# Moving one load and one request to another queue and another moment, with fewer filler matmuls, in the first wave of an attention + MLP kernel

## The chip, the cores and the metric

The kernel runs on one core of a Trainium2 chip. A core has five engines that run side by side, each with its own list of instructions: TensorE (PE, matrix products; "PEld" is its weight load), VectorE (DVE), ScalarE (ACT), GpSimd (POOL) and SyncE (SP, which only issues DMAs here). Sixteen DMA engines move data between the device's memory (HBM) and the core's on-chip memory (SBUF); matrix products land in PSUM. A DMA can be asked for by SP (its requests go through the queue that the profile calls q1, "hardware dynamic") or by POOL (q0, "software dynamic"). The metric is the device time in microseconds (us); the median of several runs counts.

## The reference

Two stages. The first is linear attention with decay over 4 batches, 8 heads, 768 positions and head size 64, in blocks of 64 positions: inside a block the scores are masked by powers of the head's decay, and between blocks a 64 x 64 state per head carries on.

```python
intra = (q_b @ k_b^T * Dmask) @ v_b
inter = (q_b * lam_pow) @ kv_state
out_b = intra + inter
kv_state = lam_block * kv_state + (k_b * rev_pow)^T @ v_b
```

The second is an MLP on the 3072 tokens of width 512 that come out, with 2048 hidden units:

```python
h = x @ w_in
g = h * sigmoid(1.702 * h)
out = g @ w_out
```

All inputs and the output are float32; the kernel computes its products in bfloat16.

## The kernel before, in words

The 768 positions of the four batches are worked off in waves, each of which gives 512 tokens to the MLP. Waves 0 and 1 (`w < ND`) are "dense": each takes 256 positions of two batches, called `c` = 0 and 1 (batch 0 and batch 1 in wave 0). Waves 2 to 5 take 128 positions of all four batches. While the MLP of one wave runs on TensorE, the attention of the next one is threaded in between.

`load_one` (L76) loads one of q, k, v of one batch in a wave, on SP's queue: 512 KB in rows of 512 B, either whole or in two halves by heads (L79). `load(0)` at L104 asks for all of wave 0, in the order k, q, v of batch 0, then k, q, v of batch 1; of these only v of batch 1 comes as a whole. The two weight matrices are loaded once, by `load_w_in` (L175, five chunks, the first two of 256 columns and three of 512) and `load_w_out` (L180, four chunks), on POOL's queue; these DMAs also turn float32 into bfloat16. As POOL is one engine with one list, its requests stand in line with its own work: casts of k of batch 1 (L480), half of the cast of v of batch 1 (L499), and the later requests for weights (L481, L500 to L503).

When a request goes out is set by hand. `gate_pool(x)` (L451) is a copy of one element of `x` on POOL: it waits until the DMA that brings `x` has landed, and so all that POOL has to do behind it waits too. `gate_sync` (L454) does the same for SP: a tiny DMA that reads `w_out_sb[1]` (L506), behind which `load(1)`, the loads of wave 1, stands.

`fill(n)` (L139) issues n matmuls of zeros, 128 x 128 by 128 x 512, whose result nobody reads. They take up TensorE's time at the start, where it would otherwise wait.

The order of the first wave is written out by hand from L457 on: powers of the decay on ScalarE, then for k and q of batch 0 a multiplication by the powers (`do_cast`, L189, line 198 in the profile), turns by TensorE (`turn_pe`, L228, line 234) with a copy out of PSUM (lines 214 and 217, for VectorE and ScalarE), then the scores (`d_scores`, L247, lines 255 and 263), the state (`d_one` and `d_state`, line 275) and the output (`d_out`, line 312, and `d_inter`, line 294). Batch 1 follows in the same way from L479 on. `mlp1_half(0, 0, 0)` (L509, line 405) is the first product with `w_in`, from its first chunk; the rest of wave 0's MLP follows in lines 405, 393 and 417.

After this the list `main` (L545) holds the MLP's pieces and `side` the attention's, each with the place in `main` ahead of which it is issued. Wave 1's k cast stands ahead of piece 19 of wave 0's MLP and its turn ahead of piece 24.

Of the kernel before, what the change touches and what calls it, by code (L numbers as in the profile page):

```python
# [24 lines left out]
def kernel(  # L25
# [13 lines left out]
    nc = tc.nc  # L39
    f32 = mybir.dt.float32  # L40
    bf16 = mybir.dt.bfloat16
    B, H, S, D = q.shape
# [31 lines left out]
    loaded = {}  # L74

    def load_one(w, c, nm, src):  # L76
        x = ld.tile([P, H, 2 * D], f32, tag=f"{nm}{c}", name=f"{nm}f")
        if w < ND:
            n = H if w or (nm == "v" and c) else H // 2  # L79
            for h in range(0, H, n):  # L80
                nc.sync.dma_start(  # L81
                    out=x[:, h : h + n],
                    in_=src[2 * w + c, h : h + n, 0 : 2 * P, :].rearrange("h (s a) d -> s h (a d)", a=2))
        else:
            nc.sync.dma_start(out=x.rearrange("p h (a d) -> p (h a) d", a=2),
                              in_=src[2 * c : 2 * c + 2, :, w * P : (w + 1) * P, :].rearrange("b h s d -> s (b h) d"))
        loaded[w, c, nm] = x

    def load(w, nms="kqv"):
        src = {"k": k, "q": q, "v": v}  # L90
        if w < ND:
            for c in range(HF):
                for nm in nms:
                    load_one(w, c, nm, src[nm])
        else:
            for nm in nms:
                for c in range(HF):
                    load_one(w, c, nm, src[nm])
# [3 lines left out]
    ones = const.tile([1, P], f32)  # L102
    nc.vector.memset(ones, 1.0)
    load(0)  # L104

    nc.scalar.preload_act_table_set("natural_log_exp_and_others")
# [29 lines left out]
    def acc(name, dt=f32, shape=None, tag="a"):  # L136
        return ps.tile(shape or [P, 4, P], dt, tag=tag, bufs={"a": 5, "mm": 3}[tag], name=name)

    def fill(n, new=None):  # L139
        if new:  # L140
            fill_ps[0] = acc("ps_fill", shape=[P, W], tag=new)
        for _ in range(n):
            nc.tensor.matmul(fill_ps[0], zero[:, 0:P], zero, start=True, stop=True)  # L143
# [31 lines left out]
    def load_w_in(j):  # L175
        c0 = sum(IN_CH[:j]) * P
        nc.gpsimd.dma_start(
            out=w_in_sb[j], in_=moe_w_in.rearrange("(kc ki) f -> ki kc f", ki=P)[:, :, c0 : c0 + IN_CH[j] * P])
# [10 lines left out]
    def do_cast(w, c, nm, eng, g=None):  # L189
        if g in (None, 0):  # L190
            cast[w, c, nm] = work.tile([P, 2, HD], bf16, tag=f"{nm}s{c}", name=f"{nm}s")
        f, x = loaded[w, c, nm], cast[w, c, nm]
        if w < ND:
            pw = {"k": kd_pow, "q": qd_pow}[nm]
            for R in (0, 1) if g is None else (g,):
                for j in range(2):
                    h = slice(4 * R + 2 * j, 4 * R + 2 * j + 2)
                    eng.tensor_tensor(x.rearrange("p a (r i j d) -> p r j i a d", i=2, j=2, d=D)[:, R, j],  # L198
                                      f[:, h].rearrange("p i (a d) -> p i a d", a=2),
                                      pw[:, h].unsqueeze(3).to_broadcast([P, 2, 2, D]), op=MUL)  # L200
        else:
            pw = {"k": k_pow, "q": q_pow}[nm]
            n = 2 * H // 4
            for j in range(2):
                eng.tensor_tensor(x.rearrange("p b (r i j d) -> p j (b r) i d", i=2, j=2, d=D)[:, j],  # L205
                                  f.rearrange("p h (a d) -> p (h a) d", a=2).rearrange("p (n j i) d -> p j n i d", j=2, i=2)[:, j],
                                  pw.rearrange("p b (r j i) -> p j (b r) i", i=2, j=2)[:, j].unsqueeze(3).to_broadcast([P, n, 2, D]),
                                  op=MUL)
# [10 lines left out]
    def cast_v(w, c, copies=(pool_copy, pool_copy)):  # L219
        f = loaded.pop((w, c, "v"))  # L220
        dst = v_sb[w % 2]
        if w < ND:
            for a in range(2):
                copies[a](dst[:, 2 * c + a], f.rearrange("p h (a d) -> p h a d", a=2)[:, :, a, :])
        else:
            copies[0](dst[:, 2 * c : 2 * c + 2].rearrange("p b h d -> p (b h d)"), f.rearrange("p h e -> p (h e)"))

    def turn_pe(w, c, nm, copy=act_copy, g=None):  # L228
        x = cast[w, c, nm]
        rr = list(range(NP)) if g is None else [2 * g, 2 * g + 1]  # L230
        t = acc("ps_t", bf16, [P, len(rr), 2, P])
        for i, r in enumerate(rr):
            for a in range(2):
                nc.tensor.transpose(t[:, i, a, :], x[:, a, r * P : (r + 1) * P], ident)  # L234
        if g in (None, 0):
            trans[w, c, nm] = work.tile([P, 2 * NP, P], bf16, tag=f"{nm}T{c}", name=f"{nm}T")
        copy(trans[w, c, nm][:, 2 * rr[0] : 2 * rr[0] + 2 * len(rr)], t.rearrange("p r a s -> p (r a) s"))
# [9 lines left out]
    def d_scores(w, c, pp, split=False):  # L247
        kT = trans[w, c, "k"]
        s2 = [acc("ps_s") for _ in range(2)]
        for i in range(2):  # L250
            r = 2 * pp + i
            for a in range(2):
                for blk, bs in enumerate((A, Z)):
                    for h, hs in enumerate((A, Z)):
                        nc.tensor.matmul(s2[h][bs, 2 * i + a, :], kT[hs, 2 * r + a, bs], q_of(w, c, hs, r, blk),  # L255
                                         start=True, stop=True)
        for h in range(2):
            sm = work.tile([P, 2, 2, P], bf16, tag="sm", bufs=8, name="sm")
            flat = s2[h].rearrange("p (i a) s -> p i (a s)", i=2)
            if split and h:  # L260
                nc.scalar.copy(sm.rearrange("p i a s -> p i (a s)"), flat)
                flat = sm.rearrange("p i a s -> p i (a s)")
            nc.vector.tensor_tensor(sm.rearrange("p i a s -> p i (a s)"), flat,  # L263
                                    mask_d.rearrange("p o a b s -> p o (a b s)").to_broadcast([P, 2, 2 * P]), op=MUL)
            masked[w, c, pp, h] = sm
# [185 lines left out]
    def gate_pool(x):  # L451
        nc.gpsimd.tensor_copy(behind_q, x)
# [4 lines left out]
    with tc.manual_schedule():  # L457
# [4 lines left out]
            nc.scalar.activation(blk_pow[rows].rearrange("p (r i) -> p r i", i=2),  # L462
                                 ln_lam[rows].rearrange("p (r j i) -> p r j i", i=2, j=2)[:, :, j, :], EXP, scale=1.0 * P)
        nc.scalar.activation(warm, q_pow[:, 0, 0:1], GELU)
        fill(5)
        for nm, copies in (("k", (dve_copy, act_copy)), ("q", (act_copy, dve_copy))):
            for g in range(2):
                do_cast(0, 0, nm, nc.vector, g)
            for g in range(2):
                turn_pe(0, 0, nm, copies[g], g)  # L470
                fill(2 if nm == "k" or g == 0 else 0)
        gate_pool(loaded[0, 0, "v"][0:1, 0, 0:1])
        load_w_in(0)
        cast_v(0, 0, (act_copy, act_copy))
        d_scores(0, 0, 0)
        fill(1)
        d_scores(0, 0, 1)
        fill(3)
        for g in range(2):  # L479
# [22 lines left out]
        for j in range(NCH):  # L502
            load_w_out(j)  # L503
        nc.gpsimd.affine_select(mask, mask, pattern=[[0, 1], [1, P]], channel_multiplier=-1, base=0,
                                compare_op=mybir.AluOpType.is_ge, fill=0.0)
        gate_sync(w_out_sb[1][0:1, 0, 0:2])  # L506
        load(1)
        d_scores(0, 1, 1, True)
        mlp1_half(0, 0, 0)  # L509
# [98 lines left out]
```

## Time and profile before

| | us |
|---|---|
| median of 5 runs | 208.13 |
| lowest and highest | 207.39, 209.78 |
| profiled execution, its own time | 208.47 |
| its span, first to last instruction | 206.8 |
| TensorE busy | 199.1 (96%) |
| VectorE busy | 89.5 (43%) |
| ScalarE busy | 86.2 (42%) |
| GpSimd busy | 16.2 (8%) |
| DMA queue of SP, share of 16 engines | 56.8% |
| DMA queue of GpSimd, share of 16 engines | 13.1% |

The times in a timeline count from the span's first instruction. A row of a chain or a timeline begins with start and duration; a bracket with an arrow tells how long the engine stood idle before, and what ended that. In a row of a DMA queue stand the packets, the megabytes written, and the time that the packets took as a share of 16 engines, which can be over 100% as packets overlap. A request for a DMA on SP or POOL has a duration too: it is the time of issuing, not of moving the data; the landing is told apart from it. Busy time of TensorE counts a matmul until its modelled end, so an engine that is 96% busy isn't at 96% of its peak.

### The profile page before, as it was taken

What the parts mean: (1) busy time and instruction counts of PE and PEld (TensorE: products, weight loads), DVE (VectorE), ACT (ScalarE), POOL (GpSimd) and SP (SyncE); (2) the same over time, 40 slices, a digit from 0 to 9 for tenths busy, and PEclk for the clock granted to TensorE, in tenths of its full rate; (3) what the DMA queues carried; (4) which work ended last, traced back from release to release, by engine and by line L of the source; (5) the groups of instructions that cost most, each with busy time, mean ns of one, the idle gap of its engine ahead of it and who ended that gap; (6) DMA issues with size and microseconds to landing.
All of it is one profiled execution on the core that took longest, in us unless ns stands there. A gap on an engine that the chain in (4) does not pass through costs nothing.

```text
span 206.8 us, 4271 instructions
## 1 busy us (share of the span) xinstructions
PE 199.1 (96%) x1806; PEld 104.5 (51%) x1830; DVE 89.5 (43%) x160; ACT 86.2 (42%) x158; POOL 16.2 (8%) x37
## 2 busy tenths in 40 slices
PE   7999999999999999999999999999999999999994
PEld 2477444467854464444464444464444454444453
DVE  1892000686951843931743841743841731100121
ACT  4877661157665030566021566021466021565000
POOL 4369000060000000000000000000000000000000
PEclk9999999999999999999999999999999999999999
DMA  5999999999899899988991379971360011100112
GB/s 146 330 238 178 176 206 239 319 310 227 182 215 172 196 276 245 236 194 196 230 270 71 103 179 229 243 216 52 101 155 0 37 68 51 51 0 0 54 51 101
DMA packets 87640, 33.82 MB, mean 164 GB/s; under 512 B 67398, under 2 KB 84678, under 8 KB 87622
## 3 DMA queue, kind: packets, MB, share of 16 engines
q1 hardware_dynamic: 82868, 29.37, 56.8%
q0 software_dynamic: 4752, 4.19, 13.1%
q8 instruction: 14, 0.23, 0.4%
q14 instruction: 4, 0.03, 0.1%
q10 hardware_dynamic: 2, 0.00, 0.0%
HBM read 27.26 MB, written 6.29 MB: 162 GB/s over the span
## 4 chain that ended last, share of the span: by engine, by line
PE 76%; DMA 15%; SPq 4%; DVE 2%; POOL 1%; issue 1%
PE ps_out L417 35%; PE ps_h L393 28%; DMA w_out<-in_moe_w_out_dram 6%; PE ps_h L405 3%; DMA vf<-in_v_dram 3%; SPq L81 3%; DMA kf<-in_k_dram 3%; PE ps_s L331 2%; PE ps_o L381 2%; DMA qT<-qs 2%; PE ps_o L368 1%; DVE o_sb L421 1%; PE ps_t L234 1%; PE ps_kv L355 1%; DVE ks L198 1%
## 5 line engine op out<-in xcount | busy, mean ns | idle before, releaser
L417 PE MATMUL ps_out<-w_out,g_sb 128*128 128x512 bf16 (+2 forms) x400 | 83.8, 362 | 1.1 <-issue 0.6
L393 PE MATMUL ps_h<-xT,w_in 128*128 128x512 bf16 x330 | 73.2, 379 | 0.3
L395 ACT ACTIVATE g_sb<-ps_h 128x512 bf16<-128x512 f32 x84 | 50.2, 597 | 45.2 <-PE ps_h L393 45.2
L417 PEld LDWEIGHTS <-g_sb 128*128 128x128 bf16 x416 | 38.2, 98 | 41.0
L393 PEld LDWEIGHTS <-w_in 128*128 128x128 bf16 x336 | 32.9, 98 | 39.2
L421 DVE COPY o_sb<-ps_out 128x512 f32<-128x512 f32 (+2 forms) x26 | 16.9, 651 | 52.4 <-PE ps_out L417 52.3
L339 DVE SCALAR_TENSOR_TENSOR sm<-ps_s,inv_pow,mask 128x512 bf16<-128x512 f32 x32 | 21.8, 743 | 27.5 <-PE ps_s L331 27.5
L385 ACT CAST xT<-ps_o 128x512 bf16<-128x512 f32 x16 | 8.2, 599 | 38.1 <-PE ps_o L381 38.1
L198 DVE TENSOR_TENSOR ks<-kf,kd_pow 128x256 bf16<-128x256 f32 x8 | 2.9, 421 | 22.6 <-DMA kf<-in_k_dram 19.3
L405 PE MATMUL ps_h<-xT,w_in 128*128 128x256 bf16 x96 | 11.4, 273 | 0.2 <-DMA w_in<-in_moe_w_in_dram 0.2
L205 DVE TENSOR_TENSOR qs<-qf,q_pow 128x512 bf16<-128x512 f32 x16 | 10.3, 686 | 0.0
L205 DVE TENSOR_TENSOR ks<-kf,k_pow 128x512 bf16<-128x512 f32 x16 | 10.3, 684 | 0.0
L405 PEld LDWEIGHTS <-w_in 128*128 128x128 bf16 x96 | 9.0, 98 | 1.9 <-DMA w_in<-in_moe_w_in_dram 0.4
L263 DVE TENSOR_TENSOR sm<-ps_s,mask_d 128x512 bf16<-128x512 f32 x14 | 8.8, 684 | 0.7 <-PE ps_s L255 0.5
L407 ACT ACTIVATE g_sb<-ps_h 128x512 bf16<-128x512 f32 x12 | 7.2, 598 | 4.3 <-PE ps_h L405 4.3
L143 PE MATMUL ps_fill<-zero 128*128 128x512 bf16 x18 | 6.8, 504 | 1.4 <-DVE zero L113 1.4
L359 DVE SCALAR_TENSOR_TENSOR kv<-kv,blk_pow,ps_kv 128x256 bf16<-128x256 bf16 x12 | 5.0, 477 | 6.0 <-PE ps_kv L355 6.0
L217 ACT COPY kT<-ps_t 128x512 bf16<-128x512 bf16 (+1 forms) x4 | 3.2, 792 | 8.2 <-PE ps_t L234 8.2
L198 DVE TENSOR_TENSOR qs<-qf,qd_pow 128x256 bf16<-128x256 f32 x16 | 5.9, 428 | 0.1
L214 DVE CAST v_sb<-vf 128x1024 bf16<-128x1024 f32 x8 | 5.3, 689 | 1.1 <-DMA vf<-in_v_dram 1.1
L331 PEld LDWEIGHTS <-kT 64*128 64x128 bf16 x128 | 3.6, 94 | 3.6 <-issue 3.6
L331 PE MATMUL ps_s<-qT,kT 64*128 64x128 bf16 x128 | 5.1, 217 | 0.1
(68 smaller groups left out, 90.6 us busy)
## 6 DMA issues: line engine op xcount, KB each, us to landing
vf<-in_v_dram SPq DMA_DIRECT2D x11, 512.0 KB, 6.4
kf<-in_k_dram SPq DMA_DIRECT2D x10, 512.0 KB, 5.6
qf<-in_q_dram SPq DMA_DIRECT2D x10, 512.0 KB, 6.6
out_dram<-o_sb SPq DMA_DIRECT2D x15, 256.0 KB, 2.0
out_dram<-o_sb SPq DMA_DIRECT2D x17, 128.0 KB, 2.4
w_out<-in_moe_w_out_dram POOLq DMA_DIRECT2D x4, 512.0 KB, 14.4
w_in<-in_moe_w_in_dram POOLq DMA_DIRECT2D x3, 512.0 KB, 8.0
kf<-in_k_dram SPq DMA_DIRECT2D x4, 256.0 KB, 3.1
```

Source lines behind the costliest of these rows:

```text
L198: eng.tensor_tensor(x.rearrange("p a (r i j d) -> p r j i a d", i=2, j=2, d=D)[:, R, j], f[:, h].rearrange("p i (a d) -> p i a d", a=2), p ...
L205: eng.tensor_tensor(x.rearrange("p b (r i j d) -> p j (b r) i d", i=2, j=2, d=D)[:, j], f.rearrange("p h (a d) -> p (h a) d", a=2).rearran ...
L263: nc.vector.tensor_tensor(sm.rearrange("p i a s -> p i (a s)"), flat, mask_d.rearrange("p o a b s -> p o (a b s)").to_broadcast([P, 2, 2 * ...
L331: nc.tensor.matmul(s2[h][:, b, :], kT[hs, (b % 2) * NP + p, :], qT[hs, (b % 2) * NP + p, :], start=True, stop=True)
L339: nc.vector.scalar_tensor_tensor(sm, s, inv_pow[:, n : n + 1], mask.to_broadcast([P, B, P]), op0=MUL, op1=MUL)
L385: nc.scalar.copy(xT[w][:, p, :], ps_o.rearrange("p b s -> p (b s)"))
L393: nc.tensor.matmul(h, w_in_sb[j][:, kc, i * P : (i + 1) * P], xT[w][:, kc, :], start=(kc == 0), stop=(kc == KC - 1))
L395: nc.scalar.activation(g_of[w][:, fc, :], h, GELU)
L405: nc.tensor.matmul(h[:, u, :], w_in_sb[j][:, kc, i * P : (i + 1) * P], xT[w][:, kc, cols], start=(kc == 0), stop=(kc == KC - 1))
L407: nc.scalar.activation(g_of[w][:, fc : fc + 2, cols], h, GELU)
L417: nc.tensor.matmul(ps_out, g_of[w][:, fc, g * P : (g + 1) * P], w_out_sb[j][:, fc % CW, c0:c1], start=(fc == 0), stop=(fc == FFC - 1))
L421: nc.vector.tensor_copy(o, ps_out)
```

## The change

Four edits, all of them in wave 0.

1. v of batch 1 is no longer loaded by SP at the start. POOL asks for it, on its own queue, right behind the request for the first chunk of `w_in` and ahead of its casts of k of batch 1.
2. The element that POOL's gate copies is no longer the first of v of batch 0 but the first of the second half of q of batch 0 (`H // 2` is where that half begins).
3. Five fillers go: two of the five ahead of the first turn, one behind the second turn of k, one behind the first turn of q, and the one between the two groups of scores.
4. `load` leaves out the tile that is now asked for by hand. No computation of the output is changed.

```diff
@@ load_one @@
-                nc.sync.dma_start(
+                (nc.gpsimd if w == 0 and c and nm == "v" else nc.sync).dma_start(
                     out=x[:, h : h + n],
@@ load @@
                 for nm in nms:
-                    load_one(w, c, nm, src[nm])
+                    if w or c == 0 or nm != "v":
+                        load_one(w, c, nm, src[nm])
@@ wave 0 @@
-        fill(5)
+        fill(3)
         for nm, copies in (("k", (dve_copy, act_copy)), ("q", (act_copy, dve_copy))):
             for g in range(2):
                 do_cast(0, 0, nm, nc.vector, g)
             for g in range(2):
                 turn_pe(0, 0, nm, copies[g], g)
-                fill(2 if nm == "k" or g == 0 else 0)
-        gate_pool(loaded[0, 0, "v"][0:1, 0, 0:1])
+                fill(2 - g if nm == "k" else 1 - g)
+        gate_pool(loaded[0, 0, "q"][0:1, H // 2, 0:1])
         load_w_in(0)
+        load_one(0, 1, "v", v)
         cast_v(0, 0, (act_copy, act_copy))
         d_scores(0, 0, 0)
-        fill(1)
         d_scores(0, 0, 1)
         fill(3)
```

## The prediction

> **What bounds the kernel now.** First the page's top and busy rows: how much of the span TensorE is not busy.
>
> ```profile
> span 206.8 us, 4271 instructions
> PE 199.1 (96%) x1806; PEld 104.5 (51%) x1830; DVE 89.5 (43%) x160; ACT 86.2 (42%) x158; POOL 16.2 (8%) x37
> ```
>
> PE is idle for 206.8 - 199.1 = 7.7 us: 1.4 before the first filler, about 3 at the tail, which the change doesn't reach, so some 3.3 are left. That is the ceiling of what earlier data can give; fewer fillers can give little besides, as PE mostly waits where they stand.
>
> Then the chain that ended last, in order of time, since the change is in the first 15 us and I must know by which way they reach the end.
>
> ```profile
> 7.95 7.11 DMA vf<-in_v_dram
> 15.05 0.06 issue
> 15.11 0.61 POOL v_sb L211
> 15.72 1.43 POOL w_in L177 x2
> 17.15 0.71 POOL w_out L181
> 17.86 13.43 DMA w_out<-in_moe_w_out_dram
> 31.30 0.02 issue
> 31.31 0.77 SPq L455
> 32.09 0.05 issue
> 32.14 5.81 DMA kf<-in_k_dram
> 37.95 0.02 issue
> 37.97 1.44 DVE ks L198 x4
> 39.41 0.05 issue
> 39.46 0.40 PE ps_t L234 x4
> ```
>
> v of batch 1 lands at 15.05; POOL casts its half, then asks for the late weights; when the second chunk of w_out lands (31.30) SP may load wave 1; its k lands at 37.95, and PE takes the casts up at 39.46. From there the chain is nearly all PE. So PE at 39.46 is the gate: what PE wins before it is lost in waiting unless the DMA chain moves too. How long PE waits there is in the timeline of PE:
>
> ```profile
> 38.79 0.40 PE L234 MATMUL ps_t<-ident,ks 128*128 128x128 bf16 x4
> 39.46 0.40 PE L234 MATMUL ps_t<-ident,ks 128*128 128x128 bf16 x4 [0.27 <-DVE ks L198]
> ```
>
> PE is 0.27 us early. A PE delay up to 0.27 before this point costs nothing; a DMA delay counts whole.
>
> Last the DMA queues, in stretches of half a microsecond: SP's queue moves 323 to 349 packets of 512 B in each from 6.0 to 12.0 (some 690 a us, about 350 GB/s), and the GpSimd queue's first packets are in 11.5 to 12.0, though its first request was issued from 8.08 to 9.03. Between 12 and 15:
>
> ```profile
> q0 software_dynamic: 864, 0.43, 110.2%
> q1 hardware_dynamic: 297, 0.14, 16.9%
> ```
>
> The engines are full from 6 to 31 us but for two dips: 88% at 13.5 to 14.0 (where 120 to 130% stands beside it), and 91% over 17.9 to 19.0 (110 to 120% beside it). In a full queue a reordering wins only such dips: about 0.15 and 0.25 us.
>
> **The change, part by part.**
>
> Fillers. Five of 20 go: two of fill(5), one behind k's second group, one behind q's first, and fill(1) between the scores. Fill(5) ends where transposes start (5.83), while the cast they need is done by 5.45; with three they start at 5.45. The vector engine gains less: kT's copy (6.33) can't start before the four casts end at 6.06, so 0.27; the q casts, 1.42, follow, and the masks start at about 8.8 instead of 9.08. ScalarE is held by its own exponentials and table load until 7.1 and gains about 0.1. So PE's lead from fillers is some 0.3 us, all before the gate at 39.46: worth 0 at the end.
>
> Against it speaks a rule. The fillers' weight loads are 0.42 us apart at 3.72 to 4.98 (3.72, 4.13, 4.55, 4.98), and after 6 us two fillers take 0.59 together, one latency of 0.38 and 0.21: PE's pace doubled between. The granted clock reads 1.00 throughout and shows nothing of it. The Trainium skill ("TensorE: Matmul & The Clock Gate", Part 1: The HAM clock gate) says that the fast clock comes after a busy window of some 3.4 us. With three fillers PE idles from about 5.1 to 5.45. By the row, the pause ahead of lam_p's matmuls (PE's weight loads stood idle 0.84 us before them) kept nothing back, and I take 0. By the rule, at worst another window at half speed: 16 transposes at 0.05 and three fillers at 0.21 more, 1.4 us, of which two groups of four transposes (0.2 each) and two scores (0.2) lie on the path, +0.6; less 0.27 at the gate and the lead below, +0 to +0.3.
>
> The gate on POOL. Before, POOL waits for v's first half, 4.50 us until 7.87. Now for q's second half: issued at 2.41, 4.4 to landing, 6.81. The 1x1 copy moves with it, and w_in0's issue starts 0.21 later, at 7.03, ending at 7.98 (its row: 0.946). Nothing but the weights and k casts is behind this wait on POOL.
>
> v's issue on POOL. The row for its cost is the weight issues, 0.746 to 0.946 us with 528 packets each (4752 over nine). v has 1024 rows of 512 B, so about 1040 packets: 0.75 if the issue is a fixed cost, 1.9 if it goes with packets at the dearest row. I take 1.5: 7.98 to 9.48. POOL's k casts began at 9.45 and had waited 0.42 for k of batch 1: so the cost is 0.03, hidden by that landing. At 1.9 it is 0.4 on POOL and on PE's transposes at 10.70 (ready 10.66, no slack), covered by the 0.27 and the lead. The late w_in requests behind the casts stay at 11.72.
>
> SP's queue. It loses one issue (7.95, 0.69 us). Nothing is behind it there until the wait on w_out at 31.3: worth 0.
>
> When first weights and v arrive. By the rule (the Trainium skill, "DMA: Bandwidth & Descriptors", Queues, rings and completion order) an engine goes round its queues packet by packet, so from about 9 us w_in0 would take half from k and q of batch 1: q's second half, due at 11.6 (6.99 + 4.6), would slip to 13 and its cast (due 12.3) by 0.8, PE by 0.5 after slack. The row says otherwise: no GpSimd packet until 11.5, and SP's queue undiminished. I take the row: k and q as before, and w_in0's packets from 10.9 (3.8 after its issue, as before) to 11.1, when SP's queue drains, v no longer being in it. 528 packets at 330 a us: 1.6 us, until 12.7, and landing some 0.5 later, 13.2 (before: 14.58). Thus the 0.2 us wait of PE for w_in at 14.65 goes. Next v, from 12.7. Its price is the unknown: no 512 B row of the GpSimd queue is in the trace. SP's 512 B rows take 16/690 = 23 ns of an engine; the GpSimd queue's cast rows 16/330 = 48 ns for 1 KB read and 16/195 = 82 ns for 2 KB. Taken as a line these two give 13 + 35 per KB, so 30 ns at 512 B. Bounds: 23 (the bytes alone) and 48 (a GpSimd packet as such); I take 30, from the same queue. So 1040 x 30/16 = 1.95 us, until 14.65, landed near 15.1: where it landed before. ACT's and POOL's v casts, d_one and what follows then keep their places; PE's next wait is v again (15.7).
>
> The sum at the gate. DMA work up to w_out's second chunk: v by GpSimd instead of SP costs 1.95 - 1.50 = 0.45 more engine time; the dip at 13.5 is filled, 0.15 less; the dip at 18 stays, as v and so the requests at 15.7 don't move. 31.30 becomes 31.6, wave 1's k and PE's transposes at 39.46 are 0.3 later. PE arrives earlier and waits longer. From there the chain is PE's own: +0.3. Span 206.8 to 207.1; the profiled run's 208.47 (1.67 around the span) to 208.77, and by the same difference the median 208.13 to **208.4**. A measurement of this kernel (207.39 to 209.78 in five runs) can hardly tell under 1% from no change.
>
> With 23 ns: no extra engine time, both dips filled (v lands by 14.7, the late requests go out 0.4 earlier): -0.4. With 48 ns: 3.1 instead of 1.5 us, +1.6 - 0.15 = +1.4.
>
> **The rivals.**
>
> *v is as cheap on GpSimd as on SP (bytes decide).* For it: GpSimd's 1 KB and SP's 512 B rows both read near 340 GB/s. Against: the line through GpSimd's own rows doesn't pass through SP's. -0.4: 207.7. If the weights were not bound by the engines, v's whole lead of up to a microsecond would pass on: 207.1.
>
> *v's packets on the GpSimd queue are dear.* One mechanism: 48 ns an engine and packet, so v lands at 16.2, after the 15.05 of now; the k load of wave 1 lands 1.4 later and PE stalls at 39.46. It decides as soon as v's packets cost over 26 ns (0.15 us of dip over 65 packets an engine), and makes the kernel slower: 209.5. For it: that queue has never moved 512 B rows here. Against: its packets' time goes with their bytes. With other v-dependent work late, up to 210.3.
>
> *The clock comes late, or k and q are halved by the round.* PE 0.5 later after slack: 208.7.
>
> *The change does nothing*: all of it is before a gate set by total bytes: 208.1, which the likeliest case can't be told from.
>
> **How the numbers follow.** Likeliest, 208.1 to 208.7: 0.45. v cheap, 207.0 to 208.0: 0.28. v dear, 209.0 to 210.5: 0.20. Late clock or halved queue, 208.5 to 209.3: 0.07. A range of 207.3 to 209.7 leaves out the far ends of both, some 0.2 with the scatter of the median. Slower by over 1% is above 210.2: the last part of the dear case and mishaps, 0.08. Faster by over 1%, under 206.05, needs 2 of the 3.3 us idle: 0.03. The rest 0.89.
>
> **What would show it.** Right: w_in's first issue near 7.0, v's on POOL for 1.5 us; k casts on POOL still near 9.5; no GpSimd packet before 10.5; w_in0 landed near 13.2, v near 15.1; w_out's second chunk near 31.6, PE's wait at 39 grown over 0.27. Fillers at 0.21 apart from 6 us on. Wrong: v landed before 14.6 or after 16; k casts on POOL after 10; PE slow after 6.5; or the wait at 39 gone, which would put the bound on PE itself.

## The result, and the profile after

The changed kernel takes 208.55 us (median of 44 runs), and the kernel before 208.55 us (79 runs in the same comparison). The ratio is 1.0009, with a 95% interval of 0.9994 to 1.0024: 0.2 us more, between 0.1 less and 0.5 more. There is no difference that can be measured. The forecast was 208.4, 0.3 us above the 208.13 of before, and it said that so little could hardly be told from no change. The profiled execution took 208.36 us, its span is 206.6 us (before: 208.47 and 206.8).

The page's first rows of the kernel after:

```profile
span 206.6 us, 4263 instructions
PE 199.3 (96%) x1802; PEld 105.1 (51%) x1825; DVE 89.5 (43%) x160; ACT 86.0 (42%) x158; POOL 17.3 (8%) x38
```

With five fillers fewer PE is busy 0.2 us longer. Something on PE got slower; that is looked for below, behind the chain. First the chain that ended last, of the kernel after, in order of time (start, duration, what):

```profile
7.17 0.44 POOL behind_q L453
7.61 0.88 POOL w_in L178
8.49 6.47 DMA vf<-in_v_dram
14.97 0.06 issue
15.03 0.61 POOL v_sb L212
...
17.78 13.59 DMA w_out<-in_moe_w_out_dram
...
32.20 5.83 DMA kf<-in_k_dram
38.03 0.02 issue
38.05 1.44 DVE ks L199 x4
39.49 0.05 issue
39.54 0.40 PE ps_t L235 x4
```

v of batch 1 travels on another queue and lands at 14.97 instead of 15.05. From there every time is that of before to 0.1 us: w_out's second chunk at 31.36 (31.30), the casts of wave 1's k at 38.05 (37.97), PE's turn of them at 39.54 (39.46). The timeline of PE at that place:

```profile
38.87 0.40 PE L235 MATMUL ps_t<-ident,ks 128*128 128x128 bf16 x4
39.54 0.40 PE L235 MATMUL ps_t<-ident,ks 128*128 128x128 bf16 x4 [0.28 <-DVE ks L199]
```

PE still waits for the casts, 0.28 us where it was 0.27.

Where did the time on PE go? The group of the fillers between 5.8 and 9.6 us, in the kernel before and in the kernel after (count, busy us, mean ns of one):

```profile
L143 PE MATMUL ps_fill<-zero 128*128 128x512 bf16 x8 | 2.8, 412 | 0.0
```

```profile
L144 PE MATMUL ps_fill<-zero 128*128 128x512 bf16 x4 | 2.3, 634 | 0.0
```

A filler takes 634 ns while PE is still slow, called cold from here on, and 379 ns once it is quick (the 412 is a mean with one cold filler in it). In the kernel before PE becomes quick near 5.9 us, in the profiled execution of the kernel after only near 9.7. The granted clock is 1.00 in both and does not show it. What each lost and won is seen in PE's timeline of batch 1, here of the kernel after: scores, first product with w_in, and the beginning of PE's long stretch of products.

```profile
14.19 0.79 PE L256 MATMUL ps_s<-qT,kT 64*64 64x128 bf16 x32
14.90 1.05 PE L406 MATMUL ps_h<-xT,w_in 128*128 128x256 bf16 x8
...
17.92 0.83 PE L406 MATMUL ps_h<-xT,w_in 128*128 128x256 bf16 x6
```

Before, these three began at 13.66, 14.65 and 17.83, and the second had waited 0.20 us for w_in:

```profile
14.65 1.05 PE L405 MATMUL ps_h<-xT,w_in 128*128 128x256 bf16 x8 [0.20 <-DMA w_in<-in_moe_w_in_dram]
```

So after, the scores are 0.53 later (the cold pace), w_in is no longer waited for (it landed at 13.6 instead of 14.6), and the long stretch begins at nearly the same time, 17.92. In this pair of profiles a loss and a gain meet; and behind them stands the wait at 39.5, which would have taken a small loss up to 0.28 us, and any gain.

### The profile page after: what moved, and what is told of

The parts are those of the page before. It is cut to its first block, busy times and chain, and to the rows that moved or that the text cites. A ratio compares the mean times of both kernels' runs of the same rounds, so it can differ in the third digit from the quotient of the medians.

```text
span 206.6 us, 4263 instructions
## 1 busy us (share of the span) xinstructions
PE 199.3 (96%) x1802; PEld 105.1 (51%) x1825; DVE 89.5 (43%) x160; ACT 86.0 (42%) x158; POOL 17.3 (8%) x38
## 4 chain that ended last, share of the span: by engine, by line
PE 78%; DMA 15%; POOL 2%; DVE 2%; SPq 1%; issue 1%
PE ps_out L418 35%; PE ps_h L394 30%; DMA w_out<-in_moe_w_out_dram 7%; PE ps_h L406 3%; DMA vf<-in_v_dram 3%; DMA kf<-in_k_dram 3%; DMA qf<-in_q_dram 2%; PE ps_s L332 2%; PE ps_o L382 2%; PE ps_o L369 1%; DVE o_sb L422 1%; POOL w_in L178 1%; PE ps_t L235 1%; PE ps_kv L356 1%; SPq L81 1%
## 6 DMA issues: line engine op xcount, KB each, us to landing
w_out<-in_moe_w_out_dram POOLq DMA_DIRECT2D x4, 512.0 KB, 14.5
```

## The experiments

Two accounts were open. In the first, the gate theory, what PE wins or loses before 39.5 is absorbed by the wait for wave 1's k, which the DMA queue sets. In the second, two effects of about 0.5 us each happen to cancel. Each ratio is to the kernel before, measured beside it, with its 95% interval; 0.001 is 0.21 us. A profile shows one execution of a kernel, and those read here lie up to 1.4 us from their kernel's median, so the times in it are one draw.

### The two halves of the change

**fewer_fillers**: the kernel before with the five fillers taken out.

```diff
-        fill(5)
+        fill(3)
-                fill(2 if nm == "k" or g == 0 else 0)
+                fill(2 - g if nm == "k" else 1 - g)
         d_scores(0, 0, 0)
-        fill(1)
```

> Only the five fillers go; loads and requests as before. Gate theory (PE's transposes of wave 1's k at 39.5 are set by the DMA chain up to w_out's second chunk, so what happens to PE before is absorbed): PE may stay at half pace until about 10 and reach the scores of batch 1 some 0.5 us later, but it is at its transposes before the casts are done; wait there 0.1 to 0.3, time within 0.2 us of before. Rival (two effects that cancel: late clock costs 0.5, earlier data gain 0.5): this kernel is 0.4 to 0.6 us slower than before. Rival on the clock (its phase is by chance and not by the fillers): PE's pace doubles by 6.1 as before.

1.0006 (0.9967 to 1.0045): the 0.4 to 0.6 us of the cancelling account lie inside this interval, so the time does not decide. In this execution PE became quick during the third of the three fillers ahead of the first turn, near 4.8. Those three, here and in the profile of the kernel after:

```profile
3.73 1.26 PE L143 MATMUL ps_fill<-zero 128*128 128x512 bf16 x3
```

```profile
3.72 1.46 PE L144 MATMUL ps_fill<-zero 128*128 128x512 bf16 x3
```

Up to there the instructions of all kernels but no_fillers are the same on PE: the first filler that is left out would have begun near 5.0. So here PE was quick before anything differed, its moment is not set by the fillers alone, and this profile does not show what their absence does to a PE that is still cold. The scores of batch 1 were late nevertheless (14.10), for k of batch 1 landed late (9.8), and wave 1's k was turned without a wait.

**moves_only**: the change with all fillers of before.

```diff
-        fill(3)
+        fill(5)
-                fill(2 - g if nm == "k" else 1 - g)
+                fill(2 if nm == "k" or g == 0 else 0)
         d_scores(0, 0, 0)
+        fill(1)
```

> The gate on q, w_in's first chunk and v on the GpSimd queue as in the change, but all fillers of before. Gate theory: PE's pace doubles near 6, PE is ahead by some tenths at 18, waits longer than 0.28 at 39.5, and the time is within 0.2 us of before. Rival of cancelling effects: 0.4 to 0.6 us faster than before.

1.0000 (0.9970 to 1.0029). PE became quick near 6.6, and the long stretch begins earliest here and in two_fillers_back:

```profile
13.71 0.79 PE L256 MATMUL ps_s<-qT,kT 64*64 64x128 bf16 x32
14.43 1.05 PE L406 MATMUL ps_h<-xT,w_in 128*128 128x256 bf16 x8
...
17.45 0.61 PE L406 MATMUL ps_h<-xT,w_in 128*128 128x256 bf16 x4
```

w_in had landed at 12.7, nothing is waited for, and the long stretch begins 0.38 earlier than before. From the scores to that point are 3.74 us, as they are in the kernel after (14.19 to 17.92: 3.73) and in fewer_fillers (14.10 to 17.83): with the data there, this is the length of PE's own chain of products and copies. In the kernel before it was 4.17. So in this pair of profiles the moves are worth about 0.4 us at 17.8 us. It is not a fixed price: less_mlp, which is the kernel before up to 27 us, reached that point at 17.67 without a wait for w_in, and sp_gate_later, the same up to there, at 19.33. What the moves do change is w_in's first chunk, which landed at 12.7 to 14.5 in the four kernels that ask for it ahead of v, and at 14.3 to 16.4 in the seven with v on SP as before.

The expectation had PE wait longer at 39.5. It did not wait at all: w_out's second chunk was in by 29.2, 2.1 earlier than before, the casts of wave 1's k began at 36.58, and PE turned all of k in one go:

```profile
38.26 0.61 PE L235 MATMUL ps_t<-ident,ks 128*128 128x128 bf16 x8
```

The span of this execution is 206.0, 0.8 less than before, so here the lead, and the wait that fell away, did reach the end. The medians show none of it (208.24, and 208.16 before); but 0.4 us is a ratio of 0.998, inside this interval, so the run neither shows a gain at the end nor excludes it.

**two_fillers_back**: the change with five fillers instead of three ahead of the first turn, as before.

```diff
-        fill(3)
+        fill(5)
```

> The change, but with five fillers instead of three ahead of k's first turn; the three behind it stay away. If the 0.3 to 0.5 us of idle PE just ahead of the first turn is what kept the clock low, the pace doubles near 6 again; if the fillers behind it count, it doubles near 10 as in the change. Time within 0.3 us of before in either case by the gate theory; 0.4 faster by the rival if the clock is early.

0.9987 (0.9960 to 1.0015). PE became quick near 7, a moment that kernels with all fillers show too (4.9 to 7.9, below), so the run does not tell which fillers count. The long stretch began at 17.45 again, and this execution shows where such a lead can end:

```profile
17.45 2.84 PE L406 MATMUL ps_h<-xT,w_in 128*128 128x256 bf16 x24
20.89 3.41 PE L394 MATMUL ps_h<-xT,w_in 128*128 128x512 bf16 x15 [0.60 <-DMA w_in<-in_moe_w_in_dram]
```

w_in's third chunk landed at 20.8, and PE waited 0.60 for it: a second place, ahead of 39.5, where the weights pace PE.

**v_ahead_of_w_in**: the change with its two requests swapped.

```diff
-        load_w_in(0)
         load_one(0, 1, "v", v)
+        load_w_in(0)
```

> The change with the two requests swapped: v of batch 1 first, then w_in's first chunk. v should land about 1.5 us earlier, 13.0 to 13.7, and w_in near 15. Gate theory: the late weights are asked for earlier, but the sum of bytes up to w_out's second chunk is the same: it lands within 0.3 of 31.4, time within 0.3 us of before. Rival (v's landing is passed on through the requests for the late weights to w_out and to wave 1's k): second chunk and k over 1 us earlier, and the time 0.3 us faster with PE's wait at 39.5 gone.

0.9995 (0.9961 to 1.0030). v landed at 13.4 and w_in at 14.8, as expected. w_out's second chunk was in by 29.6, 1.8 us earlier than in the kernel after, and wave 1's k was turned without a wait, which the gate theory had not expected and the rival had. The rival's 0.3 us lie inside the interval, and moves_only had the chunk as early with the two requests in their usual order, so neither is decided. PE became quick only near 9.2 here, the scores began at 14.10, and the long stretch at 17.84: PE's own 3.74 us after the scores again.

### The wait at 39.5

**less_mlp**: the kernel before with eight products fewer between 27 and 31 us.

```diff
-        for kc in range(KC):
+        n = KC // 2 if w == 0 and fc >= 12 else KC
+        for kc in range(n):
...
-                             start=(kc == 0), stop=(kc == KC - 1))
+                             start=(kc == 0), stop=(kc == n - 1))
```

> The kernel before with 8 of wave 0's 128x512 products with w_in left out, two of the four that make up each of the hidden chunks 12 to 15 (so these chunks are other numbers), all of them between 27 and 31 us: PE has 8 x 0.216 = 1.73 us less to do, and no load, request or copy is touched. This gives PE a lead of 1.7 us ahead of the turn of wave 1's k at 39.5, more than the change ever could. Gate theory: the casts of k are as late as before (37.4 to 39.5), PE waits 1.4 to 2.0 us there instead of 0.3, and the time falls by 0 to 0.6 us. Rival (PE's time counts whole, and the gate is met by chance): 1.4 to 1.7 us faster.

0.9976 (0.9941 to 1.0010): 0.5 us less, between 1.2 less and 0.2 more, for 1.73 us less to do. The rival's 1.4 to 1.7 lie outside the interval. PE's timeline of this kernel:

```profile
20.83 8.85 PE L394 MATMUL ps_h<-xT,w_in 128*128 128x512 bf16 x40 [0.31 <-DMA w_in<-in_moe_w_in_dram]
29.57 7.93 PE L418 MATMUL ps_out<-w_out,g_sb 128*128 128x512 bf16 x36
38.45 0.40 PE L234 MATMUL ps_t<-ident,ks 128*128 128x128 bf16 x4 [0.94 <-DVE ks L198]
39.12 0.40 PE L234 MATMUL ps_t<-ident,ks 128*128 128x128 bf16 x4 [0.28 <-DVE ks L198]
```

The waits for the casts of wave 1's k have grown from 0.27 to 0.94 + 0.28 = 1.22 us, and a wait of 0.31 for w_in stands ahead of them. This is the direct view of the absorbing: work taken from PE before 39 turns into waiting there. PE went on from the turn 0.34 earlier than before (39.35, not 39.69), as wave 1's k itself had landed 0.34 earlier.

**five_fillers_more**: PE's load the other way, five fillers more ahead of the first product with w_in.

```diff
         d_scores(0, 1, 1, True)
+        fill(5, "mm")
         mlp1_half(0, 0, 0)
```

> The kernel before with five fillers more ahead of the first product with w_in, 5 x 0.216 = 1.08 us of PE. Gate theory: the first 0.27 is absorbed by the wait at 39.5, so the wait is 0 and the time 0.7 to 0.9 us longer; a little less if the pause for w_in (0.2) covers one filler more. If PE's time counts whole: 1.1. If all that lies before 39.5 is free: 0.

1.0003 (0.9977 to 1.0029): no cost, where 0.7 to 0.9 was expected; that miss is clear. In this execution the scores began early, at 13.44, the fillers ended near 15.2, and w_in had landed at 14.7: for the most part they stood where PE would have waited for w_in. The long stretch began at 18.07, 0.24 later than before, and the wait at 39.5 was 0.16. In this execution the cover for PE is thus twofold, and the first is w_in's first chunk. It is larger than the 0.2 of the profile of before, as the scores began 0.22 earlier.

**sp_gate_later** and **sp_gate_earlier**: the kernel before, with SP's loads of wave 1 held until w_out's third, or only first, chunk.

```diff
-        gate_sync(w_out_sb[1][0:1, 0, 0:2])
+        gate_sync(w_out_sb[2][0:1, 0, 0:2])
```

```diff
-        gate_sync(w_out_sb[1][0:1, 0, 0:2])
+        gate_sync(w_out_sb[0][0:1, 0, 0:2])
```

> The kernel before, with SP's gate ahead of wave 1's loads on w_out's third chunk (landing 33.95) instead of its second (31.30): 2.65 us later. Gate theory: wave 1's k lands about 2 to 2.7 later, PE's wait at its transposes grows from 0.27 to 2.3 to 2.9, and the time grows by 2 to 2.7 us. If wave 1's loads are not what sets the end, the time moves by less than 0.5.

1.0046 (1.0016 to 1.0076): 0.3 to 1.6 us slower, less than expected. The gate opened at 34.3, but the load of k then took 4.49 us instead of 5.81 and was cast from 39.66 on, 1.7 later than before, not 2.7. PE waited for those casts, 0.17 and 0.27 us, went on from the turn 1.7 later than before, and the span is 1.4 longer (208.2). The waits are short because PE came late by another cause, one that says how far the landings scatter:

```profile
16.42 1.05 PE L405 MATMUL ps_h<-xT,w_in 128*128 128x256 bf16 x8 [1.40 <-DMA w_in<-in_moe_w_in_dram]
```

Nothing was changed ahead of this row, and w_in's first chunk landed at 16.4 instead of 14.6.

> The kernel before, with SP's gate on w_out's first chunk (28.7): wave 1's loads compete with the last two w_out chunks. Gate theory: k is there 1.5 to 2.6 earlier, PE's wait of 0.27 goes and PE is its own bound from then: 0.2 to 0.4 us faster, if the last w_out chunk still comes in time (needed about 38.7, now landing at 36.5); if not, PE waits there and nothing is gained.

1.0032 (1.0002 to 1.0061): not faster, and slower by so little that, among a dozen such intervals, chance may do it. The expected 0.2 to 0.4 us of gain are out. SP's gate opened at 28.0, 3.3 earlier than before, but the load of k then took 8.7 us instead of 5.8, with the last chunks of w_out in the queue beside it. Its casts began at 37.60, 0.4 earlier than before and not 1.5 to 2.6. The wait of PE at 39 was gone in the profile (the turn of k began at 38.77 and ran through), and the profiled span, 206.2, is shorter than before. Why the median does not show that stays open.

**moves_sp_gate_earlier**: both the moves and SP's earlier gate, all fillers of before.

```diff
-        gate_sync(w_out_sb[1][0:1, 0, 0:2])
+        gate_sync(w_out_sb[0][0:1, 0, 0:2])
```

> The moves with all fillers of before, and SP's gate on w_out's first chunk: with the gate at 39.5 out of the way the earlier data should count. Gate theory: faster than the earlier gate alone by PE's lead at 18 us (0.1 to 0.5 us), 0.3 to 0.9 us faster than before.

1.0016 (0.9988 to 1.0044): no gain; the expected 0.3 to 0.9 us lie outside. Here too the load of wave 1's k was slow: asked for at 30.6, its casts began at 39.37, and PE waited for them. Its profile shows another scattered landing, q of batch 1, for which PE's turn waited through VectorE:

```profile
14.85 0.40 PE L235 MATMUL ps_t<-ident,qs 128*128 128x128 bf16 x4 [1.16 <-DVE qs L199]
```

**All these profiles together.** In thirteen of them, all but that of v_loaded_twice, PE goes on from the turn of wave 1's k at 38.7 to 41.4 us, and the spans are 205.9 to 208.2. The difference of the two is 166.8 to 167.4 in every one. What follows the turn thus takes nearly the same time, and the moment of the turn carries over to the end. In seven of the thirteen PE waited there for the casts (before and after among them), in six it came later than they did. The gate at 39.5 and PE's own arrival are about level, and which is the later one changes from execution to execution.

### Bytes in the queue, and the clock

**no_v_load**: the kernel before without the load of v of batch 1.

```diff
                 for nm in nms:
-                    load_one(w, c, nm, src[nm])
+                    if w or c == 0 or nm != "v":
+                        load_one(w, c, nm, src[nm])
+                    else:
+                        loaded[0, 1, "v"] = loaded[0, 0, "v"]
```

> The kernel before without the load of v of batch 1 in wave 0: batch 0's v tile is used in its place, so the output of that batch is another one, while all engines do the same work. 0.52 MB less in the full DMA queue, 1.5 us at 350 GB/s. New theory (TensorE is paced by the order of landings three times, at 14.4 by w_in's first chunk and v, near 20 by w_in's third chunk, at 39 by wave 1's k, so only bytes taken out of the full queue move it): w_in's first chunk lands 1.0 to 1.5 earlier, PE's main stretch (second group of half products) begins at 17.0 to 17.4 instead of 17.8, wave 1's k casts start near 36.5 instead of 38.0, PE's waits at 14.6 and 39.4 go, and the time falls by 0.4 to 0.9 us. Rival (PE's own list and the copies between its steps set 17.8): within 0.2 us of before.

0.9995 (0.9975 to 1.0016): no gain; most of the expected 0.4 to 0.9 us is outside the interval, its lower end is not. The profile is of an execution 1.4 us above the median. w_in did land 1.5 earlier in it (13.1), but PE's long stretch began at 17.97, 3.74 after its scores (14.23). And the room in the queue was not used. POOL's timeline, and the windows of this kernel between 12 and 14 us (busy us of PE, PEld, DVE, ACT, POOL with counts, clock, DMA share, GB/s):

```profile
11.84 1.55 POOL L180 DMA_DIRECT2D w_in<-in_moe_w_in_dram  x2
13.38 0.72 POOL L214 CAST v_sb<-vf 128x512 bf16<-128x512 f32 x1
```

```profile
12.00:14.00 2.00, 1.87 (x44) 1.37 (x44) 1.97 (x5) 1.23 (x5) 2.00 (x3) 1.00 0.56 69
```

The next weights are asked for from 11.84 on, behind POOL's casts, and their packets come up only at 13.5; over these 2 us the DMA engines are busy 0.56 of the time. w_out's second chunk was 1.1 later than before in this execution. Bytes taken away did not help here, since the next request was not out in time.

**v_loaded_twice**: one load more of the same size ahead of v, into a tile that nobody reads.

```diff
+            if w == 0 and c and nm == "v":
+                nc.sync.dma_start(
+                    out=again, in_=src[2 * w + c, :, 0 : 2 * P, :].rearrange("h (s a) d -> s h (a d)", a=2))
             for h in range(0, H, n):
```

> The kernel before with one load more of 0.52 MB on SP's queue ahead of v of batch 1, into a tile that nobody reads. New theory: w_in's first chunk and v land about 1.5 us later, PE waits 1.5 to 1.8 us for w_in near 14.6, wave 1's k is 1.5 later, and the time grows by 1.0 to 1.6 us. Rival as for no_v_load: under 0.4.

1.0123 (1.0088 to 1.0157): 1.8 to 3.3 us slower, more than the expected 1.0 to 1.6 and than the 1.5 us of its bytes. Where the rest comes from stays open.

**no_fillers**: no filler at all.

```diff
-        for _ in range(n):
+        for _ in range(0):
```

> The kernel before without any filler. PE's pace doubles late, if at all, before 15; its transposes and products of wave 0's attention run at half pace until then. New theory: the steps up to the scores of batch 1 are up to 1 us later (14.7 instead of 13.7), of which the wait for w_in and v hides some 0.5 and the wait at 39.5 another 0.3: 0 to 0.5 us slower. If the fillers carry the clock through the main stretch: over 1.5 us slower.

1.0072 (1.0050 to 1.0093): 1.0 to 1.9 us slower, more than the expected 0 to 0.5. PE stayed cold until about 18 us:

```profile
18.00 0.53 PE L275 MATMUL ps_kv<-v_sb,ks 64*64 64x64 bf16 x12
...
20.11 2.84 PE L405 MATMUL ps_h<-xT,w_in 128*128 128x256 bf16 x24
```

Twelve to sixteen such products take 0.37 to 0.44 us when PE is quick. The long stretch began at 20.11, 2.28 later than before, and the span grew by 1.4 (208.2): 0.9 us were absorbed, the 0.27 at 39.5 among them (PE turned wave 1's k at 40.92 without a wait). So the clock's moment is worth something at the end, once it is late enough.

Over the same thirteen profiles the moment at which PE becomes quick was: with all fillers or more, in eight profiles, from 4.9 (five_fillers_more) to 7.9 us (sp_gate_later), 5.9 in that of before; with two of five taken back 7; with five fewer 4.8 (fewer_fillers), 9.2 (v_ahead_of_w_in) and 9.7 (after); with none 18.

## Why the prediction was right, and which of its steps were not

**The gate at 39.5: right in kind, not the whole of it.** That a wait for wave 1's k absorbs what PE wins is shown by less_mlp (1.73 us of work gone, 1.22 us of waiting at that place). Before and after, the wait is the same 0.27 and 0.28 us. But it is not there in every execution (six of thirteen profiles have none), so it is neither a sure cover nor the only bound. That a DMA delay "counts whole" there failed in its first link: 2.65 us later at SP's gate made k's casts only 1.7 later, and cost 0.3 to 1.6. The prediction put PE's wait for w_in's first chunk at 0.2 us and had none for its third; the runs show 0 to 1.40 for the first, and for the third 0.60 (two_fillers_back), 0.40 (no_v_load) and 0.31 (less_mlp).

**v's price on POOL's queue: the step that was most off.** I counted 1040 packets at 30 ns and an issue of 1.5 us. The queue row of the page, before and after:

```profile
q0 software_dynamic: 4752, 4.19, 13.1%
```

```profile
q0 software_dynamic: 4896, 4.72, 13.7%
```

0.52 MB more came with 144 packets more, 128 of 4 KB and 16 small ones: this queue joined eight rows to a packet. Its issue is 0.92 us:

```profile
8.49 0.92 POOL L81 DMA_DIRECT2D vf<-in_v_dram  x1
```

From 12.5 to 13.0 it moved 57 packets, 348 GB/s: v is as cheap there as on SP, so the bytes decide. The dear case (48 ns, 209.5) is out, and the 0.45 us of extra engine time in the sum was nothing. With that price the prediction's own sum gives -0.4 us, 207.7, the case it called v cheap; this is below the measured interval: the dip near 13.5 was to be filled and only moved, and v was to land by 14.7 and did not.

**v's landing: right by accident.** 14.97 against 15.1, but not because its packets are dear. It was asked for at 8.49 instead of 7.98, most of its bytes were in by 13.5, and then the queue ran thin: POOL's packets took 79% of the engines from 13.0 to 13.5, 88% to 14.0. Its end came with that tail; why it is so long stays open. In the other runs with v on POOL's queue behind w_in it landed at 14.1, 14.4 and 15.9, two of which the prediction would have read as a sign of being wrong (before 14.6). With v on SP's queue and the usual bytes it landed between 12.9 and 16.6, so the change did not move it by more than the executions differ.

**Fillers: 0.3 us of lead was forecast, a lag of 0.5 came.** I weighed the Trainium skill's rule of a busy window (TensorE: Matmul & The Clock Gate, Part 1) against a pause in the trace of before and took the row, 0. The profile after is compatible with the rule: near 9.7 instead of 5.9 is 3.8 us, about one window of 3.4. Its other statement, that the window runs free of the kernel, fits the 4.8 to 7.9 of ten profiles, a spread of 3.1 us with the same instructions up to 5.0. In both profiles of kernels with three fillers in which PE was still cold when it stood idle ahead of the first turn (0.26 and 0.27 us), it became quick later than in any of those ten, at 9.2 and 9.7. That the pause is what did it is argued from the rule; two profiles do not show it. The size at the scores, 0.53, was the +0.6 of that branch; its +0 to +0.3 at the end lies inside the measured interval.

**POOL's queue behind SP's: right, with a wrong delay.** The prediction took 3.8 us from issue to first packet, "to 11.1, when SP's queue drains". After, POOL's packets come up in 10.0 to 10.5, some 2.4 to 2.9 us after the issue began and just as SP's fall. With moves_only the request goes out at 6.81, and between 9 and 10 us there is still no packet of POOL's:

```profile
q1 hardware_dynamic: 689, 0.34, 117.3%
```

In every profile the first packets of POOL's queue came as SP's thinned, at about 10 without v on SP and at 10.5 to 12 with it. The Trainium skill's rule of a round between the queues, packet by packet (DMA: Bandwidth & Descriptors, Queues, rings and completion order), isn't seen here: SP's queue went on at 344 GB/s. Whether POOL's packets were ready to go by then no view shows.

**The sum.** +0.45 for v's packets was 0; -0.15 for a dip was about 0, since the dip only moved; the gate at 31.6 came at 31.36. What was left is 0.1 us, and no change. That the forecast came so close is in part luck: its two wrong terms, +0.45 and -0.15, added up to less than a measurement can tell. What was right is the reason it gave for a small change: an early lead of some tenths can be lost in waiting at 39.5. The second account is not excluded. Its gain and loss are there in single profiles (0.38 at 17.8 us, 0.53 at the scores), but neither half of the change, run alone, moves the time by what a measurement here can tell; whether a share of either reaches the end stays open.

## What to carry to other kernels

Ask of an earlier landing which of its consumer's other inputs is then the latest, and go on asking downstream: here some tenths of a microsecond of earlier data ended, in one execution or another, in the engine's own chain of copies at 17.8, in a chunk of weights at 20 and in the next wave's load at 39. A single profile of a stage that is paced by DMA landings shows one draw of them (the same load landed between 14.3 and 16.4 us), so a wait of 0.2 us in it is neither a price nor a cover to count on. Fillers that look idle can be what makes TensorE quick; how long they must be is told by removing them in steps, and over several executions.

## What the runs showed of the hardware that was not expected

- Rows of 512 B that lie side by side in SBUF went as packets of 4 KB on POOL's queue (144 packets for 0.52 MB) and as 512 B packets on SP's (689 for 0.34 MB). Both moved near 345 GB/s.
- From the start of a request on POOL to its first packets about 1.7 us passed (11.84 to 13.5 in no_v_load), 0.75 of them in issuing it, while the DMA engines ran down from 0.86 busy (12.0 to 12.5) to 0.11 (12.5 to 13.0).
- The moment at which PE becomes quick differs by up to 3 us between executions with the same fillers (4.9 to 7.9), and the granted clock of the profile, 1.00, does not show it.
